# Chunk attention and a Swish feed-forward in one kernel: pieces of v, w_in and w_out, the first block in 128-token pieces, and a sum on VectorE

## Chip, cores and metric

The kernel runs on one core of one Trainium2 chip. The metric is the device time of the program in microseconds (us). Three runs of the kernel before gave 278.85 us as their median, from 278.25 to 279.86. The engines are TensorE (PE), VectorE (DVE), ScalarE (ACT), GpSimd (POOL) and SyncE (SP); POOL and SP also issue the DMAs.

## What is computed

Attention over separate chunks of 64 tokens, for 8 batches, 8 heads, 576 tokens and head size 64 (9 chunks a batch), and then a feed-forward layer with a Swish whose slope differs from column to column, on 4608 tokens of width 512 with a hidden width of 2048:

```python
scores = scale * np.matmul(q_c, k_c.transpose(0, 1, 2, 4, 3))   # per chunk of 64
attn = exp(scores - max); attn = attn / (sum(attn) + 1e-09)
x = matmul(attn, v_c)            # 4608 tokens x 512
h = x @ w_in                     # 512 x 2048
g = h * (1.0 / (1.0 + np.exp(-beta * h)))
return (g @ w_out).astype(np.float32)
```

All inputs and the output are float32 in memory; the loads cast to fp16 on the way.

## The kernel before, in words

The tokens are cut into 9 blocks of 512 (`BLK`). For every block there are four attention tiles of 128 tokens, two chunks each; 16 hidden units `m` of 128 columns; and 4 x 128 output rows.

**Attention.** `emit_T` turns q and k of a batch on VectorE (line 136, four transposes a batch). `emit_sc(g)` does the scores of four chunks on TensorE and their exp on ScalarE (lines 168, 177). `emit_pv(i)` multiplies with v (line 198; v carries a column of ones, which gives the sum of the weights), and normalizes on VectorE: a reciprocal and a product (lines 210 to 215). Its `where` says which PSUM banks it takes: "x" is one tile of two banks, "s" the two banks `sc0` and `sc1`, "p" two of a ring of four. In later blocks a DMA transpose from SP (line 223) lays the tile out for the feed-forward; in blocks 0 and 1 `emit_xp(i)` does that with four TensorE transposes (line 232) and a copy on ScalarE (line 235).

**First layer.** `emit_h(j, m)` (line 258) forms one hidden unit in PSUM from four matmuls over the contraction, `emit_g` applies Silu with scale beta on ScalarE (line 268). Blocks 0 and 1 use `L1_plain`: every unit directly, the first few of them in two halves of 256 tokens, so that they can start before the last tokens are ready. From block 2 on `L1` computes half of the units by a scheme with seven products (`unit`, line 311), which needs sums of w_in (`emit_sw`) and of x (`emit_xs`).

**Second layer.** Since Silu with the scale beta gives beta times too much, the rows of w_out are divided by beta (`scale_w_out`, lines 123 and 127). Block 0 uses `L2_plain` (line 510), 16 steps that each take a quarter of the contraction for one of four output tiles; hooks between the steps place the attention of block 1. Blocks 1 to 8 use seven products again (`steps_L2`, line 411): `emit_tw` forms sums of w_out, `emit_sum(j, which, part)` sums s1 to s4 of the activations in four parts each (lines 369 to 375). Parts 0 and 2 of s3 are on POOL, the rest on VectorE. A list `fill` holds the s1 and s2 parts until `dve(n)` issues n of them.

**What sets the order.** The whole order is written out by hand under `manual_schedule`; each engine runs its instructions in that order, and the framework puts in the semaphore waits. All loads but that of beta are issued by POOL, in the order in which they stand in the code: q and k of batch 0, v of batch 0, w_in in four column pieces, two pieces of w_out, q and k of batch 1, a third piece of w_out, v of batch 1, the last piece of w_out, q and k of batch 2, v of batch 2, and so on. The semaphores of POOL's loads are eight, `DMASW0` to `DMASW7`, taken in turn. Block 1's part of the main loop (`late`) places, on VectorE, the transposes of batch 3 (`T(3)`), the s3 parts 1 and 3, all s1 and s2 sums, two more transposes of batch 3, and then the normalizing of attention tiles 8 and 9; TensorE multiplies tiles 10 and 11 three products later into the same PSUM banks. In blocks 6 to 8 (`light`, j + 2 >= B) there is less attention left to place.

Of the kernel before, what the change touches and what calls it, by code (L numbers as in the profile page):

```python
# [8 lines left out]
FP32 = mybir.dt.float32  # L9
# [6 lines left out]
def kernel(  # L16
# [74 lines left out]
                    in_=src[b].rearrange("(z a) (t r) d -> (a t) z (r d)", z=2, r=RUN)[:, zs],  # L91
                )

    def load_v(b):
        t = vbuf[b % NV]
        for z in range(2):
            for hp in range(2):
                h0 = 4 * z + 2 * hp
                nc.gpsimd.dma_start(  # L99
                    out=t[64 * hp:64 * hp + 64, 2 * z:2 * z + 2, :, 0:D].rearrange(  # L100
                        "p s c d -> p (s c) d"),
                    in_=v[b, h0:h0 + 2].rearrange("s (c p) d -> p (s c) d", p=CH),
                )

    def load_w_in(g):
        n = DFF // 4
        nc.gpsimd.dma_start(
            out=w_in16[g],
            in_=moe_w_in[:, g * n:(g + 1) * n].rearrange("(k p) f -> p k f", p=128),
        )  # L110

    def load_w_out(g):
        n = NM // 4
        nc.gpsimd.dma_start(
            out=w_out16[:, g * n:(g + 1) * n].rearrange("p m r d -> p m (r d)"),
            in_=moe_w_out[g * n * 256:(g + 1) * n * 256, :].rearrange(
                "(m p r) d -> p m (r d)", p=128, r=2),
        )

    def scale_w_out(g, act=0):  # L120
        for n, kk in enumerate(range(4 * g, 4 * g + 4)):
            if n < act:
                nc.scalar.activation(
                    out=wo(kk), in_=wo(kk), func=ACTF.Copy,
                    scale=binv[:, kk % 2, kk // 2:kk // 2 + 1])
                continue
            nc.vector.tensor_scalar_mul(wo(kk), wo(kk), binv[:, kk % 2, kk // 2:kk // 2 + 1])
# [96 lines left out]
        else:  # L224
            x16_t[i] = xf

    def emit_xp(i):
        xf = x16_t.pop(i)
        j, t0 = i // 4, (i % 4) * 128
        xps = ps_s.tile([128, KDM, 128], FP16, tag=f"sc{i % 2}", name="xps")  # L230
        for kk in range(KDM):
            nc.tensor.transpose(
                out=xps[:, kk, :], in_=xf[:, kk * 128:(kk + 1) * 128], identity=ident
            )
        nc.scalar.copy(out=xt_t[j][:, :, t0:t0 + 128], in_=xps)  # L235

    def emit_idle(n, w=512, d=None):
        if d is None:
# [9 lines left out]
    hps_t = {}  # L248
    w_r = [t.rearrange("p k (m i r) -> p k m r i", r=2, i=128) for t in w_in16]

    def emit_h(j, m, c0=0, c1=BLK):
        if m == 0 and c0 == 0 and j == 0:
            gt_t[j] = gt_p.tile([128, KFF, BLK], FP16, tag="gt", name="gt")
        if c0 == 0:
            hps_t[j, m] = ps_p.tile([128, BLK], FP32, tag="p", name="hps")
        for n in range(KDM):
            e, z = n // 2, n % 2
            nc.tensor.matmul(  # L258
                out=hps_t[j, m][:, c0:c1],
                lhsT=w_r[m // 4][:, 2 * z + e, m // 2 % 2, m % 2, :],  # L260
                rhs=xt_t[j][:, n, c0:c1],
                start=(n == 0),
                stop=(n == KDM - 1),
            )

    def emit_g(j, m):
        hps = hps_t.pop((j, m))
        nc.scalar.activation(  # L268
            out=gt_t[j][:, m, :], in_=hps, func=ACTF.Silu,
            scale=beta2[:, m % 2, m // 2:m // 2 + 1],  # L270
        )
# [82 lines left out]
    def emit_m(j, m):  # L354
        emit_h(j, m)
        emit_g(j, m)
# [4 lines left out]
    def emit_sum(j, which, part):  # L361
        if j not in s_t:
            s_t[j] = [s_p.tile([128, NM, HT], FP16, tag=f"s{i}", name=f"s{i}") for i in range(4)]
        s1, s2, s3, s4 = s_t[j]
        g = gt_t[j]
        lo, hi = slice(2 * part, 2 * part + 2), slice(NM + 2 * part, NM + 2 * part + 2)
        tt = (nc.gpsimd if which == 3 and part in (0, 2) else nc.vector).tensor_tensor
        if which == 1:
            tt(out=s1[:, lo], in0=g[:, lo, dn], in1=g[:, hi, dn], op=ALU.add)  # L369
        elif which == 2:  # L370
            tt(out=s2[:, lo], in0=s1[:, lo], in1=g[:, lo, up], op=ALU.subtract)  # L371
        elif which == 3:
            tt(out=s3[:, lo], in0=g[:, lo, up], in1=g[:, lo, dn], op=ALU.subtract)  # L373
        else:
            tt(out=s4[:, lo], in0=g[:, hi, up], in1=s2[:, lo], op=ALU.subtract)
# [130 lines left out]
    def L2_plain(j):  # L506
        ops = [ps_p.tile([128, DM], FP32, tag="p", name="ops") for _ in range(4)]

        def part(kk, t):
            nc.tensor.matmul(  # L510
                out=ops[t],
                lhsT=gt_t[j][:, kk, t * 128:(t + 1) * 128],
                rhs=wo(kk),
                start=(kk == 0),
                stop=(kk == KFF - 1),
            )

        def unit(g, t):
            for kk in range(4 * g, 4 * g + 4):
                part(kk, t)  # L520
            if g < 3:
                return
            osb = osb_p.tile([128, DM], FP32, tag="osb", name="osb")
            if t % 2:
                nc.vector.tensor_copy(out=osb, in_=ops[t])
            else:
                nc.scalar.copy(out=osb, in_=ops[t])
            r0 = j * BLK + t * 128
            nc.sync.dma_start(out=out[r0:r0 + 128, :], in_=osb)

        return [lambda g=g, t=t: unit(g, t) for g in range(4) for t in range(4)]

    fill = []

# [2 lines left out]
            if fill:  # L537
                fill.pop(0)()

    def L1_plain(j, hooks, nh):  # L540
        if j:
            gt_t[j] = gt_p.tile([128, KFF, BLK], FP16, tag="gt", name="gt")
        for m in range(nh):
            emit_h(j, m, 0, HT)
            hooks.get(-1 - m, lambda: None)()
        for m in range(nh):
            emit_h(j, m, HT, BLK)
            emit_g(j, m)
        for m in range(nh, KFF):
            hooks.get(m, lambda: None)()  # L550
            emit_m(j, m)
            if j and m == 8:
                for p in (0, 2):
                    emit_sum(j, 3, p)
        if j:
            for p in range(4):
                fill.extend([lambda w=w, p=p: emit_sum(j, w, p) for w in (1, 2)])
            hooks.get(KFF, lambda: None)()

    def L1(j, hooks={}, first=None):  # L560
        gt_t[j] = gt_p.tile([128, KFF, BLK], FP16, tag="gt", name="gt")
# [8 lines left out]
            first()  # L570
        unit(j, 0, [sp(8), sp(9), sp(10)])
        unit(j, 1, [sp(11), sp(12), sp(13)])
        for p in (0, 2):
            emit_sum(j, 3, p)
        for p in (0, 2, 1, 3):
            fill.extend([lambda w=w, p=p: emit_sum(j, w, p) for w in (1, 2)])
        sp(14)()
# [6 lines left out]
    with tc.manual_schedule():  # L584
# [9 lines left out]
            )  # L594
        for t in vbuf:
            nc.vector.memset(t[:, :, :, D:D + 1], 1.0)
        load_v(0)
        make_identity(nc, ident)
        for g in range(4):
            load_w_in(g)  # L600
        load_w_out(0)
        load_w_out(1)
        load_qk(1)
        load_w_out(2)
        load_v(1)
        load_w_out(3)
        load_qk(2)

        emit_idle(4)
        for f in T_items(0):  # L610
# [13 lines left out]
        emit_sc(1, where="p")  # L624
        emit_idle(3)
        emit_pv(0, xbar=False)
        emit_pv(1, where="p", xbar=False)
        d = emit_idle(4, 256)
        emit_xp(0)
        emit_pv(2, xbar=False)  # L630
        emit_idle(2, d=d)
        emit_xp(1)
        emit_pv(3, where="p", xbar=False)
        emit_idle(3, d=d)

        L1_plain(0, {-2: lambda: emit_xp(2), -3: lambda: emit_xp(3)}, 4)
        emit_sw()
        scale_w_out(0)
        scale_w_out(1)
        emit_tw(1)  # L640
        T1 = T_items(1)
        T1[0]()
        T1[1]()
        T1[2]()
        T1[3]()
        scale_w_out(2, act=2)
        table(ACTF.Exp)
        load_v(2)
        load_qk(3)
        hooks = {  # L650
            8: lambda: [emit_sc(2, "x"), emit_sc(3)],
            10: lambda: [emit_pv(4, xbar=False), emit_pv(5, "s", xbar=False), scale_w_out(3, act=2)],
            12: lambda: [emit_pv(6, xbar=False), emit_xp(4), emit_xp(5)],
            14: lambda: [emit_pv(7, xbar=False), emit_xp(6)],
        }
        for kk, f in enumerate(L2_plain(0)):
            hooks.get(kk, lambda: None)()
# [17 lines left out]
        for j in range(1, NB):  # L675
            na = j + 1
            late = j == 1
            if late:
                L1_plain(1, {
                    -1: lambda: [emit_xp(7), table(ACTF.Silu)], 3: lambda: emit_tw(3), 4: lambda: T(2), 5: lambda: T(2),  # L680
                    6: lambda: emit_tw(2), 7: lambda: T(2), 9: lambda: T(2),
                    10: lambda: emit_tw(4), 14: lambda: T(3), 15: lambda: T(3),
                    11: lambda: [loads(1), loads_v(1)],
                    KFF: lambda: [table(ACTF.Exp), emit_sc(4, "x"), emit_sc(5)],
                }, 3)
            else:
                L1(j, {8: lambda: loads(j), 10: lambda: T(j + 2), 11: lambda: loads_v(j),
                       13: lambda: T(j + 2), 14: lambda: T(j + 2) if j + 2 < B else dve(2),
                       15: lambda: dve(2) if j + 2 >= B else None})

            def pv(n, where):
                if na < NB:
# [80 lines left out]
```

## Time and profile before

| | |
|---|---|
| Median of 3 runs | 278.85 us (278.25 to 279.86) |
| Profiled execution | 278.5 us, span 276.7 us, granted clock 0.999 |
| First v-dependent product after its wait | at 14.76 us |
| Block 0: first hidden unit starts, last ends | 18.30, 33.41 us |
| Attention tile 4 on TensorE | at 43.28 us |
| Block 1's first layer starts | at 50.23 us |
| Block 1's last product ends | at 80.7 us |
| A later block (block 5) | 27.76 us |

The profile is that of one execution. Its page gives the busy time of each engine, the span in 40 slices, and the chain of work that ended last. The timeline gives each instruction's start and duration in us from the start of the span, its engine, the line of the code, the operation, the tile written and the tile read with shape and type; in brackets stands the idle time of the engine just before it and what released it. "POOL DMA_DIRECT2D" is POOL's time to issue a load, not the transfer. Names are cut: `wi` is w_in, `hps` a hidden unit in PSUM, `gt` the activations, `x` and `xp` attention tiles, `xps` their transposes, `vb` v, `s` the sums.

### The profile page before, as it was taken

To read this page: it belongs to the slowest core of one execution; us is meant where nothing else is said; L and a number is where in the kernel's file an instruction comes from. 1 tells how busy PE (TensorE), PEld (TensorE's weight loads), DVE (VectorE), ACT (ScalarE), POOL (GpSimd) and SP (SyncE) were. 2 spreads that over 40 slices of the span, in tenths; PEclk is the share of its full clock that TensorE was granted. 3 is DMA by queue.
4 is the path that set the end of the run, shared out by engine and by line. 5 is a ranking of instruction groups with operands and counts; after the bars stand their busy time and mean duration, and the time that the engine had idled before them with its cause. 6 is when DMAs were issued, how large, how long until landed. Compare 5 with 4: busy or idle time off the path is not lost.

```text
span 276.7 us, 8206 instructions
## 1 busy us (share of the span) xinstructions
PE 263.9 (95%) x3513; PEld 189.0 (68%) x3513; DVE 218.4 (79%) x425; ACT 163.5 (59%) x276; POOL 102.6 (37%) x108
## 2 busy tenths in 40 slices
PE   2789999999999999999999999999999999999995
PEld 0355454647786688668866886688667866787684
DVE  2772655879698998899889988996789768996874
ACT  2249746789167836783678367835783478216820
POOL 8733252190118620862086206620251035013500
PEclk9999999999999999999999999999999999999999
DMA  6999999999668933892389234923203320232013
GB/s 104 176 207 211 211 182 208 213 241 190 69 143 153 153 59 116 163 154 55 115 164 157 52 111 85 75 53 107 76 2 63 93 76 0 60 98 76 2 38 115
DMA packets 69588, 31.99 MB, mean 116 GB/s; under 512 B 53680, under 2 KB 63920, under 8 KB 69552
## 3 DMA queue, kind: packets, MB, share of 16 engines
q0 software_dynamic: 44960, 18.35, 54.7%
q1 hardware_dynamic: 24448, 12.99, 17.2%
q8 instruction: 27, 0.44, 0.7%
q10 hardware_dynamic: 144, 0.13, 0.1%
q14 instruction: 9, 0.07, 0.1%
HBM read 36.71 MB, written 9.44 MB: 167 GB/s over the span
## 4 chain that ended last, share of the span: by engine, by line
PE 82%; DVE 8%; DMA 4%; POOL 2%; issue 1%; ACT 1%; DVEq 0%; ACTq 0%; POOLq 0%
PE hps L258 25%; PE oA L411 17%; PE wA L311 9%; PE wX L311 6%; PE oD L411 5%; PE ops L510 5%; PE oC L411 4%; PE oB L411 4%; DMA vb<-in_v_dram 3%; DVE x L215 2%; PE scx L168 2%; PE sc L168 2%; DVE s L369 1%; PE x L198 1%; DMA xt<-x 1%
## 5 line engine op out<-in xcount | busy, mean ns | idle before, releaser
L258 PE MATMUL hps<-xt,wi 128*128 128x512 f16 (+1 forms) x380 | 85.2, 363 | 0.3 <-ACT xt L235 0.2
L268 ACT ACTIVATE gt<-hps,beta 128x512 f16<-128x512 f32 x88 | 57.4, 682 | 20.0 <-PE hps L258 19.9
L258 PEld LDWEIGHTS <-wi 128*128 128x128 f16 x380 | 37.1, 98 | 29.0 <-issue 0.7
L411 PEld LDWEIGHTS <-s 128*128 128x128 f16 x496 | 47.5, 98 | 6.6 <-DVE s L371 0.5
L411 PE MATMUL oA<-tw,s 128*128 128x256 f16 x368 | 44.4, 273 | 0.1
L411 PEld LDWEIGHTS <-gt 128*128 128x128 f16 x384 | 36.2, 98 | 6.6
L422 ACT COPY u<-oA 128x512 f32<-128x512 f32 x24 | 14.0, 585 | 43.9 <-PE oA L411 43.9
L99 POOL DMA_DIRECT2D vb<-in_v_dram x32 | 27.5, 880 | 9.2 <-DMA wi<-in_moe_w_in_dram 5.5
L319 DVE COPY u<-wA 128x512 f32<-128x512 f32 x42 | 28.6, 681 | 2.5 <-PE wA L311 2.5
L342 POOL TENSOR_TENSOR t<-u,w 128x512 f32<-128x512 f32 x14 | 17.9, 1276 | 32.6 <-DVE u L319 32.6
L480 POOL TENSOR_TENSOR o<-t,o 128x512 f32<-128x512 f32 x7 | 8.9, 1270 | 52.3 <-ACT o L477 52.3
L311 PEld LDWEIGHTS <-sw 128*128 128x128 f16 x224 | 21.9, 98 | 9.1 <-issue 0.6
L449 POOL TENSOR_TENSOR w<-u,u 128x512 f32<-128x512 f32 x7 | 9.8, 1406 | 43.8 <-ACT u L422 22.5
L373 POOL TENSOR_TENSOR s<-gt 128x512 f16<-128x512 f16 x16 | 20.3, 1287 | 9.5 <-ACT gt L268 9.5
L136 DVE STREAM_TRANSPOSE qT<-qu 128x576 f32<-128x576 f32 x16 | 20.0, 1249 | 4.7 <-DMA qu<-in_q_dram 4.7
L136 DVE STREAM_TRANSPOSE kT<-ku 128x576 f32<-128x576 f32 x16 | 19.9, 1242 | 3.9 <-DMA ku<-in_k_dram 3.9
L369 DVE TENSOR_TENSOR s<-gt 128x512 f16<-128x512 f16 x32 | 20.6, 645 | 0.0
L311 PEld LDWEIGHTS <-wi 128*128 128x128 f16 x168 | 16.4, 98 | 4.9
L371 DVE TENSOR_TENSOR s<-s,gt 128x512 f16<-128x512 f16 x32 | 18.1, 567 | 1.1
L322 ACT ACTIVATE gt<-c,beta 128x512 f16<-128x512 f32 x28 | 18.6, 716 | 0.3
L168 PEld LDWEIGHTS <-kT 32*64 32x64 f16 x1152 | 11.7, 109 | 9.9 <-DVE kT L136 6.4
L582 ACT ACT_TABLE_LOAD x14 | 18.0, 1283 | 0.2
(87 smaller groups left out, 403.1 us busy)
## 6 DMA issues: line engine op xcount, KB each, us to landing
out_dram<-osb SPq DMA_DIRECT2D x21, 256.0 KB, 3.0
vb<-in_v_dram POOLq DMA_DIRECT2D x32, 144.0 KB, 7.6
qu<-in_q_dram POOLq DMA_DIRECT2D x7, 576.0 KB, 7.2
ku<-in_k_dram POOLq DMA_DIRECT2D x7, 576.0 KB, 9.2
out_dram<-o SPq DMA_DIRECT2D x14, 256.0 KB, 2.2
wi<-in_moe_w_in_dram POOLq DMA_DIRECT2D x4, 512.0 KB, 11.9
w_out<-in_moe_w_out_dram POOLq DMA_DIRECT2D x4, 512.0 KB, 15.9
qu<-in_q_dram POOLq DMA_DIRECT2D x2, 288.0 KB, 5.3
```

Of the source, the lines that this page charges most:

```text
L99: nc.gpsimd.dma_start(out=t[64 * hp:64 * hp + 64, 2 * z:2 * z + 2, :, 0:D].rearrange("p s c d -> p (s c) d"), in_=v[b, h0:h0 + 2].rearrang ...
L136: nc.vector.transpose(out=dst[b][:, z].rearrange("p t r e -> p (t r e)").bitcast(FP32).rearrange("p (t r) -> p r t", r=RUN), in_=src[b][:, ...
L168: nc.tensor.matmul(out=sc[a % 2][o0:o0 + 64, z, c, :], lhsT=kk[:, cb * CH:(cb + 1) * CH, e], rhs=qq[:, cb * CH:(cb + 1) * CH, e], start=(e ...
L258: nc.tensor.matmul(out=hps_t[j, m][:, c0:c1], lhsT=w_r[m // 4][:, 2 * z + e, m // 2 % 2, m % 2, :], rhs=xt_t[j][:, n, c0:c1], start=(n == ...
L268: nc.scalar.activation(out=gt_t[j][:, m, :], in_=hps, func=ACTF.Silu, scale=beta2[:, m % 2, m // 2:m // 2 + 1],)
L311: nc.tensor.matmul(out=bank[b][:, i, :], lhsT=a[:, kk, q, i, :], rhs=rhs[:, kk, :], start=(first and i == 0 and kk == 0), stop=(kk == 1), ...
L319: nc.vector.tensor_copy(out=sb[nm], in_=bank[b])
L322: nc.scalar.activation(out=gt_t[j][:, m, cols], in_=src, func=ACTF.Silu, scale=beta2[:, m % 2, m // 2:m // 2 + 1],)
L369: tt(out=s1[:, lo], in0=g[:, lo, dn], in1=g[:, hi, dn], op=ALU.add)
L371: tt(out=s2[:, lo], in0=s1[:, lo], in1=g[:, lo, up], op=ALU.subtract)
L373: tt(out=s3[:, lo], in0=g[:, lo, up], in1=g[:, lo, dn], op=ALU.subtract)
L411: nc.tensor.matmul(out=bank[name][:, i, :], lhsT=a[:, kk, i * 128:(i + 1) * 128], rhs=b[:, kk, :], start=(first and i == 0 and n == 0), st ...
```

## The change

- **v of batches 0 and 1.** `load_v` takes a range of chunks. Of batch 0 chunks 0 to 7 are loaded first, in eight loads (one for each of the eight heads) in place of four; chunk 8 follows in four loads after the fifth w_out piece. Of batch 1 chunks 0 to 6 follow in eight loads and chunks 7 and 8 in eight more, behind the last piece of w_out.
- **w_in.** The first column piece is loaded in two halves of the contraction.
- **w_out.** The last piece is loaded in two halves; the steps of `L2_plain` that use it become eight of half the size, and its scaling is placed in two hooks.
- **q and k of batch 1** are loaded in two halves each, and stand behind two pieces of w_out as before.
- **Block 0's first layer** (`L1_first`): the first four hidden units are formed in 128-token pieces and, for the first two pieces, in halves of the contraction; the token transposes stand between them, the last one copied by VectorE. Units 4 and 5 use the banks `sc0` and `sc1`, units 6 and 7 the two banks of one "x" tile. The Silu table is loaded ahead of the last two pieces. Three idle matmuls are left out.
- **Attention of block 1** moves to later and different hooks of `L2_plain`, all four tiles in the "x" banks; the last token transpose of block 1 moves there too, and block 1's first layer is no longer begun in halves.
- **s3** parts 0 and 2 are on VectorE in blocks 6 to 8, issued in the hooks 14 and 15 of the first layer, each after two of the `fill` sums.

```diff
-    def load_v(b):
+    def load_v(b, c0=0, c1=NCB):
...
+                if c1 - c0 == NCB:
+                    pairs = [(o.rearrange("p s c d -> p (s c) d"),
+                              v[b, h0:h0 + 2].rearrange("s (c p) d -> p (s c) d", p=CH))]
+                elif c1 - c0 == 1:
+                    pairs = [(o[:, :, c0], i[:, :, c0])]
+                else:
+                    pairs = [(o[:, e, c0:c1], i[:, e, c0:c1]) for e in range(2)]
+                for dst, src in pairs:
+                    nc.gpsimd.dma_start(out=dst, in_=src)
...
-        tt = (nc.gpsimd if which == 3 and part in (0, 2) else nc.vector).tensor_tensor
+        pool = which == 3 and part in (0, 2) and j + 2 < B
+        tt = (nc.gpsimd if pool else nc.vector).tensor_tensor
...
+    def L1_first():
+        gt_t[0] = gt_p.tile([128, KFF, BLK], FP16, tag="gt", name="gt")
+
+        def part(t, ns, m_last=False):
+            for m in range(4):
+                emit_h(0, m, t * 128, (t + 1) * 128, ns)
+                if m_last:
+                    emit_g(0, m)
+
+        part(0, (0, 1))
+        emit_xp(1)
+        emit_pv(3, where="s", xbar=False)
+        part(1, (0, 1))
+        part(0, (2, 3))
+        emit_xp(2, "x")
+        part(1, (2, 3))
+        emit_xp(3, eng=nc.vector)
+        table(ACTF.Silu)
+        part(2, range(KDM))
+        part(3, range(KDM), True)
+        for m in range(4, 6):
+            hps_t[0, m] = ps_s.tile([128, BLK], FP32, tag=f"sc{m % 2}", name="hps")
+        hx = ps_x.tile([128, 2, BLK], FP32, tag="x", name="hx")
+        hps_t[0, 6], hps_t[0, 7] = hx[:, 0], hx[:, 1]
+        for m in range(4, KFF):
+            emit_m(0, m)
...
-        for p in (0, 2):
-            emit_sum(j, 3, p)
+        if j + 2 < B:
+            for p in (0, 2):
+                emit_sum(j, 3, p)
...
-        load_v(0)
+        load_v(0, 0, 8)
         make_identity(nc, ident)
-        for g in range(4):
+        load_w_in(0, slice(0, KDM, 2))
+        load_w_in(0, slice(1, KDM, 2))
+        for g in range(1, 4):
             load_w_in(g)
         load_w_out(0)
-        load_w_out(1)
-        load_qk(1)
         load_w_out(2)
-        load_v(1)
-        load_w_out(3)
+        load_qk(1, split=True)
+        load_w_out(4)
+        load_v(0, 8, NCB)
+        load_v(1, 0, 7)
+        load_w_out(6, 1)
+        load_w_out(7, 1)
+        load_v(1, 7, NCB)
         load_qk(2)
...
-        L1_plain(0, {-2: lambda: emit_xp(2), -3: lambda: emit_xp(3)}, 4)
+
+        L1_first()
         emit_sw()
-        scale_w_out(0)
-        scale_w_out(1)
+        scale_w_out(range(0, 4))
+        scale_w_out(range(4, 8))
+        for f in T_items(1):
+            f()
+        scale_w_out(range(8, 12), act=2)
         emit_tw(1)
...
         hooks = {
             8: lambda: [emit_sc(2, "x"), emit_sc(3)],
-            10: lambda: [emit_pv(4, xbar=False), emit_pv(5, "s", xbar=False), scale_w_out(3, act=2)],
-            12: lambda: [emit_pv(6, xbar=False), emit_xp(4), emit_xp(5)],
-            14: lambda: [emit_pv(7, xbar=False), emit_xp(6)],
+            11: lambda: [emit_pv(4, xbar=False), scale_w_out((12, 13), act=1)],
+            12: lambda: [emit_pv(5, xbar=False), emit_xp(4)],
+            14: lambda: [scale_w_out((14, 15), act=1), emit_pv(6, xbar=False), emit_xp(5)],
+            16: lambda: [emit_pv(7, xbar=False), emit_xp(6)],
+            18: lambda: [emit_xp(7), table(ACTF.Silu)],
         }
...
-                       13: lambda: T(j + 2), 14: lambda: T(j + 2) if j + 2 < B else dve(2),
-                       15: lambda: dve(2) if j + 2 >= B else None})
+                       13: lambda: T(j + 2), 14: lambda: T(j + 2) if j + 2 < B else [dve(2), emit_sum(j, 3, 0)],
+                       15: lambda: [dve(2), emit_sum(j, 3, 2)] if j + 2 >= B else None})
```

## The prediction

> **What bounds the kernel now.** I read the page's busy shares first, then the chain of waits, then the timelines of POOL, VectorE (DVE) and TensorE (PE) over the first 80 us, and last those of VectorE and TensorE around 205 us.
>
> ```profile
> PE 263.9 (95%) x3513; PEld 189.0 (68%) x3513; DVE 218.4 (79%) x425; ACT 163.5 (59%) x276; POOL 102.6 (37%) x108
> DMA  6999999999668933892389234923203320232013
> ```
>
> TensorE is busy 95% of the span, so only its holes can be won. The DMA row is at 9 in slices 2 to 10 (a slice is 6.9 us): to about 62 us the loads are one unbroken stream. In the chain the first long step is "6.09 8.63 DMA vb<-in_v_dram"; from then on it is nearly all TensorE.
>
> The timeline of POOL shows who feeds that stream (start, duration, idle before it and its releaser):
>
> ```profile
> 2.50 0.55 POOL L89 DMA_DIRECT2D qu<-in_q_dram  x1
> 3.54 3.46 POOL L99 DMA_DIRECT2D vb<-in_v_dram  x4
> ...
> 10.67 0.74 POOL L107 DMA_DIRECT2D wi<-in_moe_w_in_dram  x1 [0.86 <-DMA ku<-in_k_dram]
> 11.73 0.70 POOL L114 DMA_DIRECT2D w_out<-in_moe_w_out_dram  x1 [0.31 <-DMA vb<-in_v_dram]
> ...
> 32.71 0.71 POOL L89 DMA_DIRECT2D qu<-in_q_dram  x1 [2.38 <-DMA qu<-in_q_dram]
> 35.48 0.70 POOL L89 DMA_DIRECT2D ku<-in_k_dram  x1 [2.06 <-DMA ku<-in_k_dram]
> 37.99 0.98 POOL L99 DMA_DIRECT2D vb<-in_v_dram  x1 [1.81 <-DMA w_out<-in_moe_w_out_dram]
> ```
>
> Load number n waits for load n-8: the 12th (last w_in piece) for the 4th, the 13th for the 5th, and so on. So eight loads are in flight at most, and POOL issues one only when the eighth before it has landed. An issue costs 0.55 us (128 rows), 0.70 to 0.76 (256 and 512 rows) or 0.86 (1152 rows, v), back to back.
>
> The timeline of VectorE shows where the stream's end matters:
>
> ```profile
> 59.25 1.26 DVE L136 STREAM_TRANSPOSE qT<-qu 128x576 f32<-128x576 f32 x1 [0.28 <-DMA qu<-in_q_dram]
> 62.16 1.26 DVE L136 STREAM_TRANSPOSE kT<-ku 128x576 f32<-128x576 f32 x1 [1.65 <-DMA ku<-in_k_dram]
> ...
> 69.64 0.21 DVE L213 RECIPROCAL rd<-x 128x8 f32<-128x8 f32 x1 [0.23 <-PE xp L198]
> ...
> 73.83 0.21 DVE L213 RECIPROCAL rd<-x 128x8 f32<-128x8 f32 x1 [2.16 <-PE x L198]
> ```
>
> VectorE waits for k of batch 3 at 62.16, then works without a hole (transpose, sums, two transposes) until it normalizes the first attention pair of block 2 from 69.64 to 71.67. TensorE needs those PSUM banks back at 73.46, for the second pair. If k lands late by d, VectorE first uses up its 0.23 us of idle, then the 1.9 us up to TensorE's need: **TensorE loses d - 2.15 us**.
>
> The last view, VectorE and TensorE in block 6:
>
> ```profile
> 204.42 1.27 DVE L371 TENSOR_TENSOR s<-s,gt 128x512 f16<-128x512 f16 x1
> 205.61 1.37 DVE L369 TENSOR_TENSOR s<-gt 128x512 f16<-128x512 f16 x1
> 207.02 0.43 DVE L371 TENSOR_TENSOR s<-s,gt 128x512 f16<-128x512 f16 x1
> ```
>
> ```profile
> 209.56 0.21 PE L198 MATMUL xp<-vb,et 64*64 64x65 f16 x1 [0.17 <-DVE x L215]
> 210.11 0.32 PE L198 MATMUL xp<-vb,et 64*64 64x65 f16 x15 [0.33 <-DVE x L215]
> ```
>
> While POOL computes its two s3 parts (204.05 to 206.70) a sum takes VectorE 1.27 or 1.37 us; beside an idle POOL 0.43. TensorE then waits for VectorE.
>
> **s3 on VectorE in blocks 6 to 8: -1.5 us.** Block 5 starts at 164.38 and lasts 27.76 us, block 6 28.57 (+0.81). Block 7 lasts 27.25 with 1.2 us less score work, so +0.69. VectorE takes on two parts of 0.4 us each and is freed of two stretched sums (0.9 us each), and starts the normalizing 0.9 us earlier. Block 8 shows no such wait: 0. The upper bound is those 1.5 us, the lower 0 (if VectorE's queue, not POOL, makes it late). I take 1.5, since the stretched rows stand directly ahead of the wait.
>
> **The front: -0.2 us.** v of batch 0 loses 1 chunk of 9, but its four loads become eight, and four of these wait for the four q and k loads. The last goes out after k landed at 10.43: by 11.4, landing about 14.1 (a v load issued alone takes 4.1 us from issue, 0.86 of that issue and about 0.9 data at the 155 GB/s of the 9 to 13 us stretch; so 2.3 plus 0.4 of data). Before, it was 14.7; the scores' exp lets the first matmul start at 14.00 in any case. The identity (0.6 us on POOL) and w_in are now queued behind these waits: the first w_in half is issued at 12.1 to 12.75, so the DMA is without work for about 1 us, and every later load comes 1.1 - 0.4 = 0.7 us later. The halves land near 16.2 and 17.4; the first 128 tokens are transposed at 16.4. The 128-column matmuls take as long in sum as before (32 of 0.109 us become 64 of 0.055, the rate of the four xps transposes in 0.22). The second attention tile must wait for the copy of xps, 0.6 us, and hidden units 0 to 3 end near 21.6. Silu starts at 21.2, after the table (1.28), at 0.6 us each. Here the change adds a wait: units 6 and 7 share one PSUM tile, and the order of the changed kernel shows unit 7's matmul waiting for unit 6's Silu, the seventh, done at 21.2 + 7 x 0.6 = 25.4, while TensorE is there at 24.2. Units 8 to 15 are queued behind it. Nine units of 0.864 from 25.4 end at 33.2, before at 33.41. Bounds: 1.4 us gained without that wait, 0.5 lost if v lands at 14.9.
>
> **The load stream: +4.0 us.** The fifth w_out load (rows 8 to 11) lands 0.7 later than the 37.8 of the ACT row that used it: 38.4, give or take 0.5. When it lands, before had issued all of v1, w_out, q and k of batch 2. Now POOL still has 15 small issues ahead of q of batch 2: five pieces of v1, two halves of w_out, eight tails of v1. Before's trace has no v piece: 128 rows of q cost 0.55, 1152 rows of v 0.86. I take 0.70 for the five pieces (448 rows, between), 0.55 for the halves and the tails (128 rows, the nearest row). Together 3.5 + 1.1 + 4.4 = 9.0 us, 0.60 each. q of batch 2 is issued by 38.4 + 0.25 + 9.0 + 0.7 = 48.35, its data moves 0.8 later (the first load: issue ends 1.98, data from about 2.75): 49.1. Before it moved at 42.8, when the last w_out piece was through. The data in between is only some 5 us of DMA time, so the DMA stands idle about 4 us and more. k of batch 3 comes 6.2 late: 6.2 - 2.15 = **+4.0**. Bounds: issues that cost nearly nothing give +0; all at 0.86 give d = 10.1 and +8.
>
> The remaining edits add no work: three idle matmuls go (0.65 us, inside the front's stretch), the last token transpose moves from block 1's first layer into block 0's second (0.22 us of TensorE either way), tw(1) behind batch 1's transposes on VectorE (1.22 us; next needed at tw(2), over 10 us later).
>
> The same queue makes v1's last piece land near 44.7 (before by 41.8) where attention tile 4 is due at 43.9, and the first w_out half near 46. TensorE waits about 1 us for the one and 0.5 for the other; VectorE's scaling of rows 13 and 15 stands ahead of the normalizing of tiles 5 and 6 and holds it too. All this, and the 0.2 of the front, is covered by the larger wait at 73 us and is not added.
>
> The Trainium skill speaks against the pieces too: "DMA: Bandwidth & Descriptors", Rules for kernel authors, says to gather many small transfers into one large, since under 64 KB one pays mostly overhead; the tails are 16 KB. Taken to the letter (a small load issued at a whole load's price) the sum would be about +6 instead of +2.5. The row of 0.55 beside that of 0.86 says that size does count, though less than in proportion.
>
> **Sum.** 4.0 - 1.5 = +2.5. The profiled execution took 278.5 us (span 276.7 and 1.8 around it): 281.0; its own time stands 0.35 below the median of 278.85. From both I take **281.2**.
>
> **Rivals.**
> - **Issues follow size, the stream keeps up** (faster). If a small issue costs 0.3 us or less, d = 15 x 0.3 - 2.8 = 1.7 stays under 2.15, nothing is lost at 73 us, and 0.2 to 0.4 of the front and 1.5 of the tail remain: 278.85 - 1.9 = 276.9. For it: 9 times the rows cost only 1.6 times the time, so row counts below 128 are unseen. Against it: no issue in the trace is under 0.53.
> - **They cancel.** At 0.45 us an issue, d = 4, loss 1.8, gain 1.5 to 1.8: 278.9.
> - **The s3 move does nothing** because VectorE has the same work in sum; with the forecast's loss 278.85 + 4.0 = 282.8. Against it: the rows of 1.27 beside 0.43.
>
> **Chances.** Forecast 0.50 (its own range 280.3 to 282.3), issues by size 0.25 (276.4 to 277.4), cancelling 0.17 (277.5 to 280.2), s3 without gain 0.08 (282.3 to 283.5). What can be told from no change is 0.5%, 1.4 us. So faster 0.25, same 0.17, slower 0.58. The range is 276.5 to 283.2: both signs, and the price per issue from 0.3 to 0.73.
>
> **What would show it.** Right: POOL issuing without a hole from 38.4 to 48; q's and k's transposes of batches 2 and 3 waiting for DMA for several us, k of batch 3 starting near 68; a hole in TensorE of 3 us or more near 74 to 77; one near 24.5 at unit 7; sums of 0.4 us near the end of block 6 and no wait for VectorE there. Wrong: small v issues of 0.3 us, or batch 3's k before 64.

## The result, and the profile after

| | before | after |
|---|---|---|
| Median | 278.62 us (278.25 to 279.86, 4 runs) | 286.83 us (285.11 to 288.66, 4 runs) |
| Ratio to before | | 1.029 (95% interval 1.021 to 1.036) |
| Profiled execution, its span, granted clock | 278.5, 276.7 us, 0.999 | 287.46, 285.5 us, 0.982 |
| Block 0: first hidden unit, end of first layer | 18.30, 33.25 us | 16.80 (one matmul) and 18.90, 37.05 us |
| k of batch 3 transposed | 62.16 us | 73.26 us |
| TensorE's product behind attention tiles 10 and 11 | 73.84 us | 82.78 us |
| Block 2's first product | 80.71 us | 91.67 us |
| From there to the end | 196.0 us | 193.8 us |

The kernel became 2.9% slower; 281.2 was forecast. In the profiled execution it is 11.0 us behind when block 2 begins, and gets 2.2 us back later.

The page of the kernel after, the row of the granted clock and that of the DMA engines' busy share, in 40 slices of 7.1 us:

```profile
PEclk9988999999978999999999999999999999999999
DMA  6999999799993892499249944854401620152013
```

The unbroken run of nines of the kernel before is gone: the DMA row has a 7 in slice 8 and a 3 in slice 13 (the slices from 50 and 86 us). And the clock row, full everywhere before, has two dips.

POOL's timeline (start, duration, idle before and its releaser):

```profile
10.75 0.68 POOL L109 DMA_DIRECT2D vb<-in_v_dram  x1 [0.78 <-DMA ku<-in_k_dram]
...
11.96 3.70 POOL L113 DMA_DIRECT2D wi<-in_moe_w_in_dram  x5
...
40.06 3.59 POOL L109 DMA_DIRECT2D vb<-in_v_dram  x5 [1.90 <-DMA w_out<-in_moe_w_out_dram]
43.60 1.18 POOL L119 DMA_DIRECT2D w_out<-in_moe_w_out_dram  x2
44.71 4.27 POOL L109 DMA_DIRECT2D vb<-in_v_dram  x7
49.54 0.59 POOL L109 DMA_DIRECT2D vb<-in_v_dram  x1 [0.56 <-DMA w_out<-in_moe_w_out_dram]
50.96 0.70 POOL L89 DMA_DIRECT2D qu<-in_q_dram  x1 [0.82 <-DVE w_out L132]
```

The 15 small issues stand where they were predicted, ahead of q of batch 2, and cost 9.6 us. The chain of waits (start, length, what) follows that queue to TensorE:

```profile
24.31 15.46 DMA w_out<-in_moe_w_out_dram
...
44.71 5.71 DMA vb<-in_v_dram
...
56.62 16.62 DMA ku<-in_k_dram
...
73.26 1.26 DVE kT L141
...
82.84 3.32 PE oA L420 x15
```

From the third load of w_out (rows 8 to 11, which the texts ahead call the fifth piece) over the v tails (q of batch 2 is eight loads behind one of them) to k of batch 3, its transpose, VectorE's sums, and the product on TensorE. TensorE's own timeline:

```profile
16.80 0.23 PE L265 MATMUL hps<-xt,wi 128*128 128x128 f16 x1 [0.30 <-DMA wi<-in_moe_w_in_dram]
18.90 0.56 PE L265 MATMUL hps<-xt,wi 128*128 128x128 f16 x7 [1.86 <-DMA wi<-in_moe_w_in_dram]
...
29.28 1.02 PE L265 MATMUL hx<-xt,wi 128*128 128x512 f16 x4 [0.98 <-ACT gt L276]
...
81.32 0.43 PE L203 MATMUL x<-vb,et 64*64 64x65 f16 x16 [2.28 <-DVE x L220]
...
82.78 3.60 PE L420 MATMUL oA<-tw,s 128*128 128x256 f16 x16
```

The two halves of w_in were issued from 11.96 us on, one behind the other (KB, us from issue to landing):

```profile
wi<-in_moe_w_in_dram POOLq DMA_DIRECT2D x1, 256.0 KB, 4.8
wi<-in_moe_w_in_dram POOLq DMA_DIRECT2D x1, 256.0 KB, 6.2
```

So the first half landed near 16.8 us and the second, issued 0.7 later, near 18.9, and TensorE's second matmul began when the second half was there. By the code that matmul reads only the first half. The wait for w_in at 18.90 was not foreseen; the wait of unit 7 and the one at 81.32 were. The last row of TensorE's timeline is a product of 16 matmuls that ran at half clock; before:

```profile
73.84 1.92 PE L411 MATMUL oA<-tw,s 128*128 128x256 f16 x16
```

VectorE in block 6 shows the s3 parts on it and no stretched sum ahead of the normalizing:

```profile
214.78 0.42 DVE L380 TENSOR_TENSOR s<-s,gt 128x512 f16<-128x512 f16 x1
215.12 0.42 DVE L382 TENSOR_TENSOR s<-gt 128x512 f16<-128x512 f16 x1
```

### The profile page after: what moved, and what is told of

It is laid out like the page before. It is cut to its first block, busy times and chain, and to the rows that moved or that the text cites. A ratio compares the mean times of both kernels' runs of the same rounds, so it can differ in the third digit from the quotient of the medians.

```text
span 285.5 us, 8264 instructions
## 1 busy us (share of the span) xinstructions
PE 266.9 (93%) x3530; PEld 190.7 (67%) x3530; DVE 215.3 (75%) x430; ACT 163.2 (57%) x276; POOL 107.2 (38%) x126
## 4 chain that ended last, share of the span: by engine, by line
PE 69%; DMA 19%; POOL 5%; DVE 4%; issue 2%; ACT 0%; DVEq 0%; POOLq 0%; ACTq 0%
PE oA L420 19%; PE hps L265 17%; PE wA L319 9%; DMA ku<-in_k_dram 8%; PE wX L319 6%; DMA w_out<-in_moe_w_out_dram 5%; PE oB L420 5%; PE oC L420 5%; PE oD L420 4%; DMA wi<-in_moe_w_in_dram 3%; DMA vb<-in_v_dram 2%; POOL vb L109 2%; PE scx L173 1%; PE sc L173 1%; PE x L203 1%
## 5 line engine op out<-in xcount | busy, mean ns | idle before, releaser
L276 ACT ACTIVATE gt<-hps,beta 128x512 f16<-128x512 f32 x86 | 56.4, 681 | 19.9 <-PE hps L265 19.9
L420 PEld LDWEIGHTS <-s 128*128 128x128 f16 x496 | 48.4, 100 | 7.0 <-DVE s L380 0.5
L420 PE MATMUL oA<-tw,s 128*128 128x256 f16 x368 | 45.9, 279 | 0.0
L109 POOL DMA_DIRECT2D vb<-in_v_dram x52 | 39.1, 779 | 13.6 <-DMA w_out<-in_moe_w_out_dram 6.2
L378 DVE TENSOR_TENSOR s<-gt 128x512 f16<-128x512 f16 x32 | 17.7, 554 | 0.0
L319 PE MATMUL wA<-xs,sw 128*128 128x256 f16 x112 | 16.8, 273 | 0.0
L380 DVE TENSOR_TENSOR s<-s,gt 128x512 f16<-128x512 f16 x32 | 15.6, 488 | 1.1
```

Of the source, the lines that this page charges most:

```text
L109: nc.gpsimd.dma_start(out=dst, in_=src)
L276: nc.scalar.activation(out=gt_t[j][:, m, :], in_=hps, func=ACTF.Silu, scale=beta2[:, m % 2, m // 2:m // 2 + 1],)
L319: nc.tensor.matmul(out=bank[b][:, i, :], lhsT=a[:, kk, q, i, :], rhs=rhs[:, kk, :], start=(first and i == 0 and kk == 0), stop=(kk == 1), ...
L420: nc.tensor.matmul(out=bank[name][:, i, :], lhsT=a[:, kk, i * 128:(i + 1) * 128], rhs=b[:, kk, :], start=(first and i == 0 and n == 0), st ...
```

## The experiments

Two theories were set against each other first. **Stream theory**: the many small loads make q and k of batches 2 and 3 late. **First-layer theory**: the late first half of w_in and the new first layer of block 0 carry the loss. Ratios are to runs of the kernel before on the same chip.

### One part of the change at a time

**The kernel after with before's loads.** In the list of loads:

```diff
-        load_v(0, 0, 8)
+        load_v(0)
...
-        load_w_in(0, slice(0, KDM, 2))
-        load_w_in(0, slice(1, KDM, 2))
-        for g in range(1, 4):
+        for g in range(4):
...
-        load_v(0, 8, NCB)
-        load_v(1, 0, 7)
-        load_w_out(6, 1)
-        load_w_out(7, 1)
-        load_v(1, 7, NCB)
+        load_v(1)
+        load_w_out(6)
```

(and q and k of batch 1 whole).

> The changed kernel with the loads of before (v of a batch in four whole loads, w_in in four pieces, w_out in four, q and k of batch 1 unsplit, order of before); all else as changed. Stream theory (POOL's many small loads, eight in flight, make k of batch 3 late and TensorE waits for VectorE): k of batch 3 is there at about 62 again instead of 73, no wait at attention tile 10, no halved clock, sums on VectorE keep their 1.6 us: about 277 us. First-layer theory (the 128-token pieces, the wait of unit 7 and the moved attention of block 1 are what costs): the 3.7 us that TensorE is late at the end of block 0's first layer stay, some 281 us or more.

280.06 us, ratio 1.005 (1.002 to 1.007): most of the loss is gone, though the time is 3 us above the stream theory's figure and only 1 below the first-layer theory's.

**The kernel before with after's loads alone**: the same lines the other way.

> The kernel before with nothing changed but the loads (pieces and order of the change). Stream theory: k of batch 3 lands 10 to 11 us late, TensorE loses that minus 2.15 and about 2 us by a lower clock after its wait, nothing is given back by the sums in blocks 6 and 7: 287 to 290 us. First-layer theory: within 2 us of before, 278 to 280.

290.4 us, ratio 1.041 (1.038 to 1.044). It is 0.4 us above the stream theory's range. The loads alone make more than the whole loss, with before's first layer; k of batch 3 came at 74.39, TensorE waited 4.23 us for VectorE ahead of tiles 10 and 11, and the product behind them took 3.60 us, at half clock:

```profile
83.51 0.44 PE L203 MATMUL x<-vb,et 64*64 64x65 f16 x16 [4.23 <-DVE x L220]
84.97 3.60 PE L416 MATMUL oA<-tw,s 128*128 128x256 f16 x16
```

Attention tile 4 waited 1.73 us for v too (to 48.90), a wait that the kernel after, with its later hooks, doesn't have. The first-layer theory falls as the main cause.

**The kernel before with s3 on VectorE in blocks 6 to 8**: only the two lines of `emit_sum` and the hooks 14 and 15.

> The kernel before with only the s3 parts 0 and 2 of blocks 6 to 8 on VectorE. Stream theory makes no claim; the sums' rows say that blocks 6 and 7 get 0.8 us shorter each: 277.0 us. The rival (VectorE has the same work in sum) says no change, 278.6.

277.67 us, ratio 0.995 (0.993 to 0.997). It is the fastest of all the kernels here.

**The kernel before with `L1_first` alone** in place of `L1_plain(0, ...)`.

> The kernel before with only block 0's first layer in 128-token pieces (L1_first, with its banks and token transposes); loads, hooks and sums as before. Stream theory: the first hidden unit starts about 1 us earlier, unit 7 waits about 1 us for unit 6's Silu, the sum is within 0.7 us of before, 278 to 279.3. First-layer theory: 281 us or more.

282.91 us, ratio 1.013 (1.008 to 1.017): a miss of the stream theory, and in the range of the first-layer theory, which so holds for a part of the loss. The profile has a hole of 1.93 us in TensorE, to 72.59, between attention tiles 8 and 9, that no semaphore explains (releaser "issue"), and half the clock for 3.4 us behind it.

**The kernel with before's loads and before's first layer too**: what is left is the new places of block 1's attention, the smaller last units of block 0's second layer, and s3.

```diff
-        part(0, (0, 1))
-        emit_xp(1)
-        emit_pv(3, where="s", xbar=False)
...
+        for m in range(4):
+            emit_h(0, m, 0, HT)
+            if m in (1, 2):
+                emit_xp(m + 1)
+        for m in range(4):
+            emit_h(0, m, HT, BLK)
+            emit_g(0, m)
```

> The kernel after with before's loads and with before's first layer of block 0 (halves of 256 tokens); of the change only the new places of block 1's attention, the smaller last units of the second layer and s3 on VectorE are left. Block 0's second layer with block 1's attention takes 17.68 us in the kernel after where it took 16.98. Theory (L1_first costs what is left between s3 alone, 277.67, and the kernel with before's loads, 280.06, but for these 0.7): 278.2 to 278.6. Rival (the new places of the attention carry the rest): 279.5 to 280.2.

278.16 us, ratio 0.996 (0.995 to 0.997), at the edge of what the theory had, and not the rival's figure. So in this order of taking parts away, in us of 278.85 from the ratios: s3 -1.4, the new places +0.3 (the intervals of the two runs overlap, so it is not told from nothing), `L1_first` +2.4, the loads +6.7, in all +8.0. The parts don't simply add: put into the kernel before one at a time, the loads cost 11.3 us and `L1_first` 3.5.

### Which of the loads

**v of batch 1 whole** (`load_v(1)` ahead of the w_out halves, no tails of batch 1):

> The kernel after, but v of batch 1 in four whole loads ahead of the w_out halves. Stream theory: when the fifth w_out piece has landed near 40, POOL has 3 issues left ahead of q of batch 2 in place of 15, so that q is issued by about 43 instead of 51.7 and k of batch 3 is transposed near 64 to 65 instead of 73.3; TensorE's wait at attention tiles 8 to 11 and its low clock behind it go. What is left is the late front (+3.7 us at the end of block 0's first layer) and the gain of blocks 2 to 8 (-2.4): about 280.5 to 281.5. Rival, first-half theory (the late first half of w_in and what follows it on the queue carry the loss by themselves): 285 or more.

283.77 us, ratio 1.015 (1.011 to 1.020). q of batch 2 was issued at 43.41, k of batch 3 transposed at 67.08 with a wait of 0.47 us only, and TensorE's wait at tiles 8 to 11 is gone, as expected. The time misses the stream theory's range by 2.3 us and doesn't reach the rival's. The front cost more than 3.7: TensorE waited 3.38 us for the second half of w_in, to 20.15, the clock was half from 18.8 to 25.6 us, and block 0's first layer ended at 39.06. What the later wait had covered now shows, and so does the "issue" hole, 2.08 us here.

**v of batch 0 whole** (`load_v(0)`, no tail of batch 0):

> The kernel after, but v of batch 0 in four whole loads. Both halves of w_in are then issued before 8 us, as before, and the first layer of block 0 ends near 34.3 instead of 37.05. Stream theory: 11 small issues are left ahead of q of batch 2 in place of 15, from about 38.6: q is issued near 46, k of batch 3 is transposed near 67 to 68 (d = 5 to 6), TensorE loses 3 to 4 there, less 2.4 in blocks 2 to 8: 280 to 282, with or without 2 more for a low clock behind the wait. First-half theory: 279 to 280, as with before's loads altogether.

280.80 us, ratio 1.006 (1.004 to 1.009), inside the stream theory's range, and by its steps as far as k of batch 3. VectorE's timeline:

```profile
65.32 1.26 DVE L141 STREAM_TRANSPOSE qT<-qu 128x576 f32<-128x576 f32 x1 [3.57 <-DMA qu<-in_q_dram]
68.10 1.26 DVE L141 STREAM_TRANSPOSE kT<-ku 128x576 f32<-128x576 f32 x1 [1.53 <-DMA ku<-in_k_dram]
```

q of batch 2 was issued at 46.08 (46 expected), k of batch 3 transposed at 68.10 (67 to 68). With 15, 11 and 3 small issues ahead of it, q of batch 2 goes out at 50.96, 46.08 and 43.41. d is 5.94, for which 3.79 us of lateness are due on TensorE; its product behind tiles 10 and 11 stands 3.66 late. That this fits is partly luck: TensorE was itself late by then, from the front and a hole of 1.16 us, and waited for VectorE only some 0.3 us.

**v of both batches whole**, the halves of w_in, w_out, q and k as in the kernel after:

> The kernel after, but v of batches 0 and 1 in four whole loads each; the halves of w_in and w_out and of q and k of batch 1 stay. Stream theory (the pieces of v alone make the loss that loads make): as with before's loads altogether, 279.5 to 280.7; k of batch 3 transposed by 63 to 64. Rival (the halves of w_in and w_out carry part of it): 281.5 or more.

282.53 us, ratio 1.013 (1.010 to 1.016): a miss of the stream theory by 2 us, and in the rival's range. k of batch 3 came at 63.50, as expected, and no wait for it is left. In the profiled execution the last part of v of batch 0 let TensorE go on only at 15.71 (before: 14.76), the clock was half from 16 to 19.4 us, block 0's first layer ended at 36.10, and the "issue" hole took 2.33 us. So the pieces of v explain all of the late k, but not the whole difference to before. The rival's mechanism isn't seen: TensorE's second matmul of the first layer didn't wait for the second half of w_in here. The landing of v varies by itself: in the nine kernels that load v of batch 0 whole, its last part landed between 14.2 and 16.2 us, latest in the kernel with before's loads and first layer. Why is not known.

Nor does the loss split by batch: 286.83 with both v in pieces, 283.77 with v of batch 1 whole, 280.80 with v of batch 0 whole, 282.53 with both whole. The late front and the late k run side by side, so taking one away brings out the other.

**The first piece of w_in whole**, v in pieces:

> The kernel after, but the first column piece of w_in is loaded whole again. It tells what makes the first w_in data land at 18.7 in the kernel after (issued at 11.96) where 16.2 was predicted. Pieces theory (the four v pieces that wait for q and k leave the DMA without work at 12 to 14 us, and it comes back to its full rate of 200 GB/s only by 18): the same dip with a whole piece, the first hidden unit at 19 or later, 286 to 288.5. Rival (two halves of half the size move worse): the rate is back by 15, the first unit before 18.3, the time 1 us or more below that of the kernel after (285.5 or less).

287.27 us, ratio 1.029 (1.024 to 1.033). Stretches of 1 us of the kernel after, then of this one (start and end, the busy time of PE, PEld, DVE, ACT and POOL, clock, DMA share, GB/s):

```profile
13.00:14.00 1.00, 1.00 (x31) 0.42 (x23) 0.38 (x1) 1.00 (x4) 1.00 (x2) 1.00 0.59 83
14.00:15.00 1.00, 0.94 (x37) 0.59 (x36) 0.64 (x2) 0.55 (x2) 1.00 (x3) 1.00 1.07 106
15.00:16.00 1.00, 0.68 (x21) 0.54 (x22) 0.93 (x5) 0.25 (x1) 1.00 (x2) 1.00 0.98 114
16.00:17.00 1.00, 0.70 (x3) 0.10 (x2) 0.97 (x3) 0.34 (x1) 1.00 (x2) 1.00 1.14 155
```

```profile
13.00:14.00 1.00, 1.00 (x42) 0.65 (x31) 0.56 (x2) 1.00 (x3) 1.00 (x2) 1.00 1.02 50
14.00:15.00 1.00, 1.00 (x37) 0.52 (x35) 0.20 (x1) 0.77 (x2) 1.00 (x2) 1.00 0.64 82
15.00:16.00 1.00, 0.62 (x8) 0.34 (x6) 0.93 (x4) 0.00 (x0) 1.00 (x3) 1.00 1.25 203
```

The dip at 13 to 15 us is in both, as the pieces theory has it: the last v piece waits for k, and w_in is queued behind it. But with a whole piece the rate is back at 203 GB/s at 15 us, with halves it needs until 18; there the rival was right (first unit at 17.71, first layer's end at 34.77). What landed near 18.9 in the kernel after was the second half; the whole piece was there 1.2 us sooner.

The time did not follow. The front got 2.3 us shorter, but a w_out half landed later in this execution, and TensorE gave the gain back in block 0's second layer:

```profile
51.01 1.42 PE L519 MATMUL ops<-w_out,gt 128*128 128x512 f16 x4 [2.70 <-ACT w_out L128]
```

POOL waited 2.21 us for the same half (to 50.50), and k of batch 3 came at 74.73. By d - 2.15 the product behind tiles 10 and 11 was due 10.42 us late; it came 10.30 late, at 84.14. So k sets that product here as in the kernel after; a shorter front with everything else as it was has not been run.

### Three more waits

**Unit 7 apart from unit 6**, in the kernel with before's loads:

```diff
-        hps_t[0, 6], hps_t[0, 7] = hx[:, 0], hx[:, 1]
+        hps_t[0, 6] = hx[:, 0]
```

> The kernel after with before's loads, but unit 7 of block 0 takes a bank of the ring (that of unit 0) in place of the second bank of unit 6's tile. Theory: the wait of 1.02 us at unit 7 goes and with it 0.8 to 1.0 us: block 0's first layer ends near 33.3, time 279.0 to 279.3 against 280.06 with the shared tile. Rival (units 8 to 15 then wait for ScalarE's Silu, so the time comes back): 280.

280.09 us, ratio 1.004 (1.002 to 1.006), no gain. The wait of 1.02 us is gone from the profile, and the first layer takes 15.9 us from its first matmul instead of 17.0; but it began 1.05 us later in this execution (w_in at 18.35), so it ended at 34.23 instead of 34.34. Units 8 to 15 run without a wait for ScalarE, so the rival's mechanism is not seen either. What the wait is worth in time stays open.

**TensorE kept busy in the kernel after** ahead of tiles 10 and 11:

```diff
+        def idle_C():
+            grab("C")
+            emit_idle(10, d=bank["C"].rearrange("p a b -> p (a b)"))
...
             if late:
+                idle_C()
                 pvs(2)
```

> The kernel after, with ten idle 512-column matmuls (2.2 us) on TensorE ahead of attention tiles 10 and 11 of block 2, where it stood idle for 2.28 us; they write the free bank of product C. Theory (the halved clock in 82 to 88 us follows from TensorE standing idle there): granted clock 1.0 in that stretch, -2.3 us, 284 to 285. Rival (the low clock has another cause, or the time is bound by VectorE after the wait): clock or time as in the kernel after, 286.5 to 287.2.

287.99 us, ratio 1.031 (1.028 to 1.034): in the time, a miss by 3 us. One stretch of the kernel after, then of this one:

```profile
84.00:86.00 2.00, 2.00 (x12) 1.37 (x9) 2.00 (x6) 0.00 (x0) 0.00 (x0) 0.50 0.64 128
```

```profile
84.00:86.00 2.00, 1.44 (x34) 1.14 (x26) 1.90 (x7) 0.00 (x0) 0.00 (x0) 1.00 0.35 67
```

The clock stays full, and from the product behind tiles 10 and 11 to block 2 it takes 6.73 us instead of 8.89: 2.2 us, nearly the 2.3 that were expected. The time shows none of it. In this execution the stream was 1.5 us later (k of batch 3 at 74.74 against 73.26), and a sum on VectorE took 1.37 us. So the effect on the clock is shown, a gain in time is not.

**The stream of TensorE's instructions shifted**, in the kernel with unit 7 apart:

```diff
-        emit_idle(4)
+        emit_idle(4, d=emit_idle(36, 64))
```

> The kernel with before's loads and unit 7 apart, and 36 more idle matmuls of 64 columns on TensorE at 1 to 8.6 us, where it waits for the first q and k. They move every later instruction of TensorE 36 matmuls on in its stream. Theory (the hole of 1.7 us at 71 to 73 us that nothing in the profile releases sits at a fixed place of TensorE's instruction stream, and is long where short matmuls lie there): the hole moves from attention tile 8 back into product B ahead of it, and shrinks to 0.5 us or less as in the kernel before; time 278.6 to 279.2 against 280.09. Rival (the hole belongs to attention tile 8 or to a moment of the run): it stays in that tile, 1 us or more long, 280.

284.85 us, ratio 1.021 (1.018 to 1.025). TensorE's timeline without the 36 matmuls, then with them:

```profile
71.00 0.27 PE L203 MATMUL xp<-vb,et 64*64 64x65 f16 x12
72.98 0.22 PE L203 MATMUL xp<-vb,et 64*64 64x65 f16 x4 [1.71 <-issue]
```

```profile
71.77 1.04 PE L420 MATMUL oB<-w_out,gt 128*128 128x256 f16 x8
75.58 1.25 PE L420 MATMUL oB<-w_out,gt 128*128 128x256 f16 x8 [2.77 <-issue]
```

The hole has moved by exactly 36 matmuls: from behind the 12th of attention tile 9 (`xp`), over the 16 of tile 8 (`x`), to behind the 8th of 16 of product B (12 + 16 + 8). So it belongs to a place in the instruction stream, as the theory said. The rest of the theory failed: the hole did not shrink but grew to 2.77 us. A second one of 1.06 us appeared, to 17.82, with low clock behind both, and the clock was also half from 8 to 14.8 us, behind the added matmuls; so the time says nothing of what the hole costs.

## Why the prediction was right or wrong

The direction was right, and so was the path of the main loss, from POOL's issues over k of batch 3 and VectorE to TensorE. The step that failed is the size of the load-stream term: the prediction took k of batch 3 as 6.2 us late, and it came 11.1 late. Two costs were put at nothing beside it: `L1_first`, +2.4, and the clock behind the new wait, about +2 (inside the figure for the loads).

The forecast had +2.35 us (281.2 against 278.85), the runs +8.0. Part by part, as the runs above split it: the loads +6.7 where +4.0 stood, `L1_first` +2.4 where nothing was added (the front's -0.2 was held to be covered), the new places +0.3 where 0 stood, s3 -1.4 where -1.5 stood. That makes 5.5 of the 5.65 us that were missing; the rest is that 281.2 was set 0.15 below 278.85 + 2.5.

1. **s3, -1.5: right.** Blocks 6 and 7 became 0.81 and 0.80 us shorter in the kernel after; alone it gave 1.4 us.
2. **"TensorE loses d - 2.15 us": right.** d was 11.1; 8.95 was due, and TensorE's product came 8.94 late.
3. **The load stream, d = 6.2: the place right, the size wrong, 11.1.** The price of an issue was met: 0.72 for the five pieces (0.70), 0.59 for the halves and 0.61 for the tails (0.55), 9.6 us for the 15 (9.0). What failed lies around it. The third w_out load (rows 8 to 11) landed at 39.8 and not at 38.4 (+1.4). From 12 to 18 us the DMA moved 94, 110 and 160 GB/s in stretches of 2 us where it moved 182, 211 and 203 before; at about 210 GB/s that is an estimated 2.2 us of its work, where the prediction put down one. Behind the issues the eight-in-flight rule bit once more: POOL waited 0.56 us for a w_out half and 0.82 for a tail (+1.4; the second wait's releaser is named as VectorE, but its work had long been done and the chain leads to the tail). With the price (+0.6) q of batch 2 was out 3.3 us late. The other 1.6 us come after that: the DMA had run dry (10 GB/s at 50 to 52 us, 104 at 52 to 54), and the loads behind moved at 172 to 175 GB/s in 56 to 60, where about 210 is usual. The prediction took the data of the pieces as some 5 us of DMA time, hidden beside the issues; but from 40 to 46 us the DMA moved 46 to 104 GB/s, where whole loads of v run at 155 to 165. Its busy share stays high there, so that the row of nines does not show it. Whether issuing or moving sets that rate is not told apart.
4. **The front, -0.2: wrong, but covered.** The step "the halves land near 16.2 and 17.4" took a landing 4.1 us after the issue from a load that goes alone. The first half landed 4.8 us after its issue, near 16.8, the second 6.2 us after, near 18.9. And TensorE could use the first for one matmul only, since the second matmul waited for the second half. In five of the six kernels with halves that matmul starts within 0.05 us of the second half's landing; in the sixth both halves had landed before. By the code it reads quarter 2 of the contraction, counted 0 to 3, and the first half holds quarters 0 and 2, so its data was there. That the framework, which puts in the waits, sees the interleaved halves as overlapping would explain it, but was not tried. Unit 7's wait came as predicted, 0.98 us (1.2 foreseen). The first layer ended 3.8 us later, at 37.05. The prediction said that this is covered by the wait at 73 us. It was: ahead of that wait TensorE was 5.8 us late (75.38 against 69.57, the "issue" hole of 1.14 us included), and k put it 8.94 us late; only the larger counts.
5. **No clock effect was foreseen: about +2.** The hole of 2.28 us at 79 to 81 us was followed by half the clock to 88. From the product behind it to block 2 it took 8.89 us, before 6.87, and 6.73 with TensorE kept busy. It was part of no term.
6. **`L1_first` costs +2.4, and the sum had nothing for it.** With before's loads and L1_first the first layer ends at 34.34, without it at 34.73 (where v landed late): not much between them. The difference stands 37 us later: the "issue" hole of 1.72 us, which is absent without `L1_first`; it is the largest single difference between these two profiles ahead of block 2. All ten kernels with `L1_first` have that hole, 0.86 to 2.77 us long; the four without it have none above 0.4. That the hole makes up the 2.4 us is read from profiles and not tested. By what `L1_first` makes it long is not shown: it puts 29 matmuls more into the stream ahead of it (3542 instead of 3513 in the run with `L1_first` alone; 3530 in the kernel after, where block 1's first layer has 12 fewer), and the run with 36 more shows that the count moves its place, but not what sets its length.

The rivals: "issues follow size" and "they cancel" are refuted by the rows of 0.59 to 0.72, and "the s3 move does nothing" by the run with s3 alone (0.995). Of the rule of the Trainium skill that the prediction weighed ("DMA: Bandwidth & Descriptors", Rules for kernel authors, on many small transfers), the direction held. Read to the letter, by that text, it gave +6, nearer to the measured 8.0 than the forecast; that is luck, since its step, a small load issued at a whole load's price, did not come (0.59 to 0.72 us against 0.86).

## What to carry to other kernels

Where a queue holds a fixed number of loads in flight, as here, cutting a load into pieces can cost twice: an issue for each piece, and a stretch in which the engines move little data (46 to 104 GB/s here). Count both, up to the first large load behind them, and take the time from issue to landing from a stretch that is as empty as the one to come. If a load is cut so that work can start on its first part, see in the profile which part the first instructions wait for. And when a new wait is predicted on TensorE, allow for the clock behind it, here 0 to 2 us.

## What the runs showed of the hardware that was not expected

**The clock falls behind short holes, though not behind each.** After TensorE stood idle for 1.86 us (to 18.90) the granted clock was 0.50 from 20 to 23.4 us; after 2.28 us (to 81.32) from 81.4 to 88.2; after 1.93 us in the kernel with `L1_first` alone (to 72.59) from 73.4 to 76.8; after 1.65 us in the run with v of both batches whole (to 15.71) from 16 to 19.4. After 2.08 and 2.33 us in two others (to 78.18 and 75.47) it stayed at 1.0. The Trainium skill ("TensorE: Matmul & The Clock Gate", Part 1) gives an idle window of about 3.4 us that runs freely. The lengths of the low stretches agree with one or two such windows, and that the same hole sometimes costs nothing agrees with a free-running one; but holes of 1.65 to 2.3 us were enough here, shorter than the window.

**A hole that belongs to a place in TensorE's instruction stream.** The profile's list of DMA queues has one named "q8 instruction", with 27 transfers and 0.44 MB. In stretches of 0.2 us its transfer nearest to the hole begins 2.3 to 2.6 us before TensorE goes on, in these six kernels:

| kernel | transfer begins | TensorE goes on | hole |
|---|---|---|---|
| before | 69.0 | 71.4 | 0.4 |
| before's loads | 70.8 | 73.10 | 1.72 |
| `L1_first` alone | 70.0 | 72.59 | 1.93 |
| after | 72.6 | 75.22 | 1.14 |
| v of batch 1 whole | 75.8 | 78.18 | 2.08 |
| 36 matmuls more | 73.2 | 75.58 | 2.77 |

Counted from the start of the program, the hole stands behind 861 or 862 matmuls in all ten kernels with `L1_first`, whatever lies there: with `L1_first` alone, which has 12 matmuls more ahead of it than the kernel with before's loads, it stands ahead of the first matmul of tile 9 and not behind the 12th. In the kernel before the 0.4 us stands behind 863.

So TensorE seems to wait for its own next instructions. What sets the moment of that transfer, and with it the length of the hole, stays open; it wasn't tried.

**A starved load stream comes back slowly with small loads.** With the first w_in piece in halves the DMA needed from 13 to 18 us to get from 83 to about 200 GB/s, with a whole piece from 13 to 15. The run with v of batch 1 whole, also with halves, shows the same (80, 136, 110, 161, 122 GB/s from 13 to 18). Why is open.
